# First loads on two queues in order of use, V's ones on GpSimd, and zero-adding matmuls from the first microseconds, in a gated pair of attention blocks

## The chip, the cores and the metric

One core of one Trainium2 chip runs the whole kernel. The metric is the time of one execution on the device in microseconds (us); several executions are timed and their median is quoted. The profile is one further execution, recorded; its span runs from the first instruction to the last and is about 2 us shorter than the time on the device (697.3 against 699.36 us for the kernel before).

In the profile PE is TensorE (PEld its weight loads), ACT is ScalarE, DVE is VectorE, POOL is GpSimd, SP is SyncE. SPq and ACTq are the instruction sequencers of SP and ACT, which issue transfers.

## The reference, cut

```python
# x: 2048 x 512; 32 heads of 16; bf16 inputs
g = sigmoid((x * gate_w).sum(-1, keepdims=True))
a = softmax(q k^T / 4) v  @ A_wo     # q, k, v from x @ A_wqkv, per head
b = linear attention(q', k', v') @ B_wo   # from x @ B_wqkv, phi(t) = t+1 or exp(t)
return g * a + (1 - g) * b
```

The softmax block decides the time. Its scores are handled in 2048 units, each 128 keys by 512 queries of one head (32 heads x 16 x 4). ScalarE takes two units at a time through a true exponential; VectorE (first step) and GpSimd or VectorE (two further steps) take the others through an approximation by integer arithmetic. TensorE makes the scores, multiplies the results with V, and makes all projections between them.

## The kernel before

The program is generated. Python code holds a list of tasks and candidate instructions, a model of how long each takes and when each buffer is there, and greedily emits the candidate that the model can start first. Each engine then runs its own instructions in the order emitted, with semaphore waits.

The first loads. The number after the semaphore's count in `dma` (4500.0) is a latency, and `issue` an issue time, that only the model uses; `tw` is the time at which the model counts data as there:

```python
for k3, kk in ((1, 0), (0, 1)):          # weights of K, then of Q, first 128 columns: ACT's queue
    dma(AC, wA0[:, :, k3, :], wsrc[...], semW0[k3], 16, 4500.0, writes=[r_wA0[k3]], issue=500.0)
for tb in range(4):                      # first 512 rows of x: SP's queue
    dma(SP, xnat[:, tb, :], x2[...], semX0[tb], 16, 3500.0, writes=[r_xn[tb]], issue=500.0)
dma(SP, wA0[:, :, 2, :], ...)            # weights of V
for t in range(1, NQC):                  # the other three blocks of x, transposed by the DMA, 4 pieces each
    for cc in range(NCC):
        dma(SP, xT[...], x2[...], semXT[t], 16 * NCC, 5500.0, transpose=True, issue=1300.0)
    for h in range(2):
        r_xT[t][h].w = _Raw(semXT[t], 16 * NCC)
        r_xT[t][h].tw = SP.free + 4200.0
# ... then gate weights, all of wA, wB, the rest of x, woA, woB on SP: 5.6 MB
```

The start and the filler:

```python
emit(DV, 1000, lambda: nc.vector.memset(Vc[:, 0], 1.0), writes=r_V)   # only columns 16, 17 of 18 must be one
emit(PE, 3400, [mm(...warm...) for b in range(9)], ...)               # nine 512-column matmuls on a zero tile
...
add_task(t_x0(), ...)                    # 16 transposes of the first x block on PE, two copies back (DVE, ACT)
add_task(t_k(0, 0, fixed=3), ...)        # first block of K, then of Q
add_task(t_q(0, 0, fixed=2), ...)
...
def fill_one(start, mode):               # in a gap of PE in the model, a matmul on the zero tile
    ...
    if n < 128 or PE.free < 20000.0:     # not in the first 20 us of the model
        return False
    ... mm(ps[...], warm[:, 0:128], warm[:, 0:n], start=lone, stop=lone)
```

The softmax here doesn't subtract the row's maximum and nothing guards it: scores larger than these inputs give would overflow.

## Time and profile before

The kernel before ran in 699.15 us (median of 3, 696.23 to 700.06).

| from the page | before |
|---|---|
| PE, ACT, DVE, POOL busy | 97%, 96%, 88%, 77% |
| exponentials on ACT | 706, 656.2 us |
| chain that ended last | PE 52%, ACT 32% |

The groups of instructions on ACT from 0 to 40 us and from 40 us on, before. Columns: line, engine, operation, tiles, shapes, count; busy time and mean of one; idle time of the engine just before them and who ended it.

```profile
L747 ACT ACTIVATE P<-ps 128x1024 bf16<-128x1024 f32 x21 | 20.2, 1025 | 11.4 <-PE ps L355 11.4
...
L747 ACT ACTIVATE P<-ps 128x1024 bf16<-128x1024 f32 x686 | 637.0, 1133 | 3.0 <-PE ps L355 3.0
```

In 650 us after the start the exponentials wait for TensorE for 3.0 us in all; in the first 40 us they wait 11.4 us, besides the first 9 us. So the first 40 us are the place to look. Busy time by stretches there, before. Columns: window, its length, busy us of PE, PEld, DVE, ACT, POOL with the number of instructions, granted clock of PE (1.00 is full), busy share of the DMA engines, GB/s.

```profile
0.00:10.00 10.00, 6.63 (x57) 2.96 (x58) 6.08 (x9) 3.08 (x4) 2.76 (x17) 1.00 0.63 150
10.00:20.00 10.00, 8.11 (x107) 2.70 (x107) 7.93 (x15) 6.93 (x8) 2.03 (x2) 0.58 0.51 101
20.00:30.00 10.00, 9.18 (x183) 3.60 (x181) 8.08 (x15) 7.51 (x8) 6.58 (x8) 0.91 0.89 318
30.00:40.00 10.00, 7.96 (x173) 3.25 (x177) 6.04 (x11) 5.32 (x6) 3.10 (x5) 1.00 0.82 264
```

The clock column shows half clock in most of 10 to 20 us (0.58 on average). The clock records in the trace give its limits: half clock from 11.61 to 21.85 us. The last stretch has another cause; here are two stalls of PE in it, before, from the timeline (start, length, engine, line, operation, tiles, count, and in brackets the idle time before and what ended it):

```profile
30.32 0.29 PE L361 MATMUL ps<-wA,xT 128*32 128x128 bf16 x7 [1.05 <-issue]
37.13 0.40 PE L361 MATMUL ps<-xT,T 128*32 128x512 bf16 x4 [1.72 <-issue]
```

"issue" means that the instruction waited for nothing that the profile records.

### The profile page before, as it was taken

Reading aid. Unit: us, or ns where it says so; the run is one execution under the profiler, and the core shown is the slowest. Engines: PE = TensorE matmul, PEld = TensorE weight load, DVE = VectorE, ACT = ScalarE, POOL = GpSimd, SP = SyncE. Lnnn points to the kernel's source line nnn. Section 1 sums busy time; section 2 is a strip of 40 time slices with the busy share of each in tenths; the row PEclk is TensorE's granted clock in tenths of the full one; section 3 lists DMA queues with packets and bytes.
Section 4 is the critical chain, followed back from the end, with each engine's and each line's share of the span. In section 5 each row is a group of like instructions: output and inputs, shape, how many; then the busy total and the mean of one; then the engine's idle time right before and its main releaser. Section 6 shows DMA issues by size and latency. Waiting matters only on the chain.

```text
span 697.3 us, 24196 instructions
## 1 busy us (share of the span) xinstructions
PE 679.6 (97%) x9919; PEld 205.4 (29%) x9919; DVE 614.4 (88%) x1089; ACT 668.5 (96%) x745; POOL 536.6 (77%) x597
## 2 busy tenths in 40 slices
PE   6999999999999999999999999999999999999998
PEld 2422332222322222222233323233333322222222
DVE  7788989889998888889889999889989898999985
ACT  4789999999999999999999999999999999999995
POOL 1569788887788887774797768887788888888792
PEclk8899999999999999999999999999999999999999
DMA  5810000000000000000000000000101111000001
GB/s 129 297 61 10 9 2 10 1 10 2 2 10 2 9 3 1 10 2 10 2 10 4 2 9 2 10 2 2 32 11 35 34 31 30 16 9 17 17 17 39
DMA packets 27869, 15.97 MB, mean 23 GB/s; under 512 B 19696, under 2 KB 26736, under 8 KB 27760
## 3 DMA queue, kind: packets, MB, share of 16 engines
q1 hardware_dynamic: 26704, 14.17, 7.6%
q8 instruction: 79, 1.29, 0.8%
q10 hardware_dynamic: 1056, 0.26, 0.2%
q14 instruction: 30, 0.25, 0.1%
HBM read 6.69 MB, written 2.10 MB: 13 GB/s over the span
## 4 chain that ended last, share of the span: by engine, by line
PE 52%; ACT 32%; issue 12%; DVE 2%; POOL 1%; ACTq 0%; DVEq 0%
PE ps L355 39%; ACT P L747 32%; PE ps L361 13%; POOL Z L720 1%; ACT eb L1020 1%; DVE Vc L421 0%; DVE Zbd L1054 0%; DVE KT L899 0%; DVE Qz L414 0%; ACTq L1404 0%; DVE gnat L977 0%; DVE Z L668 0%; DVE Qz L915 0%; DVE QT L921 0%; DVE mb L1021 0%
## 5 line engine op out<-in xcount | busy, mean ns | idle before, releaser
L747 ACT ACTIVATE P<-ps 128x1024 bf16<-128x1024 f32 x706 | 656.2, 1130 | 14.4 <-PE ps L355 14.4
L720 POOL TENSOR_TENSOR Z<-Z,mcon 128x512 int32<-128x512 int32 x411 | 423.7, 1056 | 100.3 <-DVE Z L668 65.4
L668 DVE TENSOR_SCALAR Z<-ps 128x512 int16<-128x512 f32 x637 | 427.0, 683 | 59.8 <-PE ps L355 53.6
L355 PE MATMUL ps<-Qz,KT 32*128 32x512 bf16 x2048 | 277.7, 387 | 5.7 <-ACT P L747 2.7
L355 PE MATMUL ps<-Z,Vc 128*17 128x512 bf16 x1911 | 277.6, 382 | 0.8 <-DVE T L985 0.5
L355 PE MATMUL ps<-P,Vc 128*17 128x512 bf16 x1411 | 256.6, 383 | 0.0
L355 PEld LDWEIGHTS ps<-Qz,KT 32*128 32x128 bf16 x2048 | 68.7, 91 | 267.4 <-ACT P L747 243.1
L725 DVE TENSOR_SCALAR Z<-Z 128x1024 int16<-128x1024 int16 x227 | 91.2, 435 | 0.5
L355 PEld LDWEIGHTS ps<-Z,Vc 128*17 128x17 bf16 x1911 | 63.6, 88 | 76.4 <-issue 48.4
L355 PE MATMUL ps<-warm 128*32 128x512 bf16 (+14 forms) x693 | 75.8, 333 | 1.4 <-POOL warm L406 1.4
L355 PEld LDWEIGHTS ps<-P,Vc 128*17 128x17 bf16 x1411 | 58.2, 88 | 52.5 <-issue 42.2
L361 PE MATMUL ps<-xT,wA 128*32 128x512 bf16 x512 | 45.7, 396 | 1.1 <-DVE xT L877 1.1
L1024 POOL TENSOR_TENSOR phiK<-eb,mb 128x512 bf16<-128x512 f32 x32 | 41.2, 1287 | 6.7 <-DVE Z L668 2.5
L952 POOL TENSOR_SCALAR Vc<-Vc 128x576 bf16<-128x576 bf16 x32 | 21.7, 680 | 15.0 <-DVE Vc L949 10.6
L1023 POOL TENSOR_SCALAR eb<-eb 128x512 f32<-128x512 f32 x32 | 19.8, 619 | 11.2 <-DVE Z L725 2.9
L355 PEld LDWEIGHTS ps<-warm 128*32 128x32 bf16 (+1 forms) x693 | 22.6, 95 | 18.8 <-issue 12.3
L985 DVE STREAM_TRANSPOSE T<-ps 128x512 f32<-128x512 f32 x32 | 22.7, 710 | 3.9 <-PE ps L361 2.1
L361 PE MATMUL ps<-wA,xT 128*32 128x128 bf16 x1024 | 23.1, 226 | 1.9 <-issue 1.1
L1008 POOL TENSOR_TENSOR T<-T,rg 128x256 bf16<-128x256 f32 x31 | 19.5, 628 | 5.4 <-DVE Z L668 1.8
L361 PE MATMUL ps<-woB,xnat 128*32 128x512 bf16 x256 | 23.3, 381 | 0.1
L1021 DVE TENSOR_SCALAR mb<-ps 128x512 f32<-128x512 f32 x32 | 21.8, 681 | 1.9 <-ACT eb L1020 0.5
L361 PE MATMUL ps<-wB,xT 128*32 128x512 bf16 x256 | 23.4, 382 | 0.0
(80 smaller groups left out, 313.5 us busy)
## 6 DMA issues: line engine op xcount, KB each, us to landing
Qz<-QT SPq DMA_DIRECT2D x120, 16.0 KB, 1.8
wA<-in_A_wqkv_dram SPq DMA_DIRECT2D x1, 1536.0 KB, 7.0
wB<-in_B_wqkv_dram SPq DMA_DIRECT2D x1, 1536.0 KB, 11.9
xnat<-in_A_x_dram SPq DMA_DIRECT2D x3, 512.0 KB, 13.1
out_dram<-outt SPq DMA_DIRECT2D x12, 128.0 KB, 1.7
xnat<-in_A_x_dram SPq DMA_DIRECT2D x4, 128.0 KB, 3.1
woA<-in_A_wo_dram SPq DMA_DIRECT2D x1, 512.0 KB, 9.4
woB<-in_B_wo_dram SPq DMA_DIRECT2D x1, 512.0 KB, 9.2
```

Of the source, the lines that this page charges most:

```text
L355: return lambda: nc.tensor.matmul(o, lhsT=l, rhs=r, start=start, stop=stop, skip_group_check=sg)
L361: h = nc.tensor.matmul(o[32 * j:32 * j + 32], lhsT=l[:, 32 * j:32 * j + 32], rhs=r, start=start, stop=stop, skip_group_check=True)
L668: return C(DV, 400, 533 * n + 74, lambda: nc.vector.tensor_scalar(o, i, ZB, 0.0, op0=ALU.add, op1=ALU.max), [r_bank[b] for b in bks], r_Z[ ...
L720: return C(PO, 400, 70 + 484 * n, lambda: nc.gpsimd.tensor_tensor(Z[:, z, 0:512 * n].bitcast(I32), Z[:, z0, 0:512 * n].bitcast(I32), mcon[ ...
L725: return C(DV, 450 if hot else 300, 69 + 134 * n, lambda: nc.vector.tensor_scalar(Z[:, z, 0:512 * n], Z[:, z0, 0:512 * n], float(m), None, ...
L747: return C(AC, 500, 427 * n + 49, lambda: nc.scalar.activation(P[:, slot, 0:512 * n], bank(b0, n), ACT.Exp, scale=ESC), [r_bank[b0 + k] fo ...
L952: yield po(690, lambda k=k: nc.gpsimd.tensor_scalar(Vc[:, k, vs].rearrange("p a b c -> p (a b c)"), Vc[:, 0, vs].rearrange("p a b c -> p ( ...
L985: yield dv(607, lambda: nc.vector.transpose(T1[:, a, :], bank(7)), [r_bank[7]], [r_T1[a]])
L1008: yield po(640, lambda: nc.gpsimd.tensor_tensor(t2[:, :, 16 * par:16 * par + 16], t1[:, :, 0:16], rg[:, a, :].unsqueeze(2).to_broadcast([1 ...
L1021: yield dv(607, lambda: nc.vector.tensor_scalar(mb[:, i, :], bank(b), 0.0, 1e-6, op0=ALU.max, op1=ALU.add), [r_bank[b], r_eb[i]], [r_mb[i]])
L1023: yield po(640, lambda: nc.gpsimd.tensor_scalar(eb[:, i, :], eb[:, i, :], 1.0, 0.0, op0=ALU.min, op1=ALU.max), [r_eb[i]], [r_eb[i]])
L1024: yield po(1300, lambda: nc.gpsimd.tensor_tensor(dst_ap, eb[:, i, :], mb[:, i, :], ALU.add), [r_eb[i], r_mb[i]], dst_res)
```

## The change

Its intent: the first x block, then the weights, arrive in the order in which they are used; the transposed loads start earlier, with more truthful latencies told to the model; VectorE is freed of a long memset; Q is projected before K so that Q's scaling overlaps; TensorE is kept active by zero-adding matmuls from 4.5 us of the model on. Core of the diff:

```diff
-        for k3, kk in ((1, 0), (0, 1)):
-            dma(AC, wA0[:, :, k3, :], ..., 4500.0, ..., issue=500.0)
-        for tb in range(4):
-            dma(SP, xnat[:, tb, :], ..., 3500.0, ..., issue=500.0)
-        dma(SP, wA0[:, :, 2, :], ..., 4500.0, ..., issue=500.0)
+        for E, tbs in ((SP, (0, 1)), (AC, (2, 3))):
+            for tb in tbs:
+                dma(E, xnat[:, tb, :], ..., 3300.0, ..., issue=450.0)
+        for k3 in (0, 1):
+            dma(AC, wA0[:, :, k3, :], ..., 3300.0, ..., issue=450.0)
         for t in range(1, NQC):
             for cc in range(NCC):
-                dma(SP, xT[...], ..., 5500.0, transpose=True, issue=1300.0)
+                dma(SP, xT[...], ..., 3900.0, transpose=True, issue=1300.0)
+            if t == 1:
+                dma(SP, wA0[:, :, 2, :], ..., 3500.0, ..., issue=450.0)
             for h in range(2):
-                r_xT[t][h].tw = SP.free + 4200.0
+                r_xT[t][h].tw = SP.free + 2900.0
...
-        emit(DV, 1000, lambda: nc.vector.memset(Vc[:, 0], 1.0), writes=r_V)
+        for p in range(NVQ):
+            emit(PO, 200, lambda p=p: nc.gpsimd.memset(Vc[:, 0, p]...[:, :, 16:18], 1.0), writes=[r_V[p]])
...
-        emit(PE, 3400, [mm(...) for b in range(9)], ...
+        emit(PE, 3000, [mm(...) for b in range(8)], ...
...
+        add_task(t_q(0, 0, fixed=2), -1, -1, "Q0,0")
         add_task(t_k(0, 0, fixed=3), -1, -1, "K0,0")
-        add_task(t_q(0, 0, fixed=2), -1, -1, "Q0,0")
...
-            if n < 128 or PE.free < 20000.0:
+            if n < 128 or PE.free < 4500.0:
```

More of the change, by code (lines that the diff above doesn't have):

```diff
@@ L380, in bass_gated_mix__mha_block__linear_attn_block__prompt_kernel @@
         out_fill = [0] * 6
-        for k3, kk in ((1, 0), (0, 1)):
-            dma(AC, wA0[:, :, k3, :], wsrc[:, :, k3 * D:k3 * D + 128], semW0[k3], 16, 4500.0, writes=[r_wA0[k3]], issue=500.0)
-        for tb in range(4):
-            dma(SP, xnat[:, tb, :], x2[128 * tb:128 * (tb + 1), :], semX0[tb], 16, 3500.0, writes=[r_xn[tb]], issue=500.0)
-        dma(SP, wA0[:, :, 2, :], wsrc[:, :, 2 * D:2 * D + 128], semW0[2], 16, 4500.0, writes=[r_wA0[2]], issue=500.0)
+        for E, tbs in ((SP, (0, 1)), (AC, (2, 3))):
+            for tb in tbs:
+                dma(E, xnat[:, tb, :], x2[128 * tb:128 * (tb + 1), :], semX0[tb], 16, 3300.0, writes=[r_xn[tb]], issue=450.0)
+        for k3 in (0, 1):
+            dma(AC, wA0[:, :, k3, :], wsrc[:, :, k3 * D:k3 * D + 128], semW0[k3], 16, 3300.0, writes=[r_wA0[k3]], issue=450.0)
         for t in range(1, NQC):
@@ L389, in bass_gated_mix__mha_block__linear_attn_block__prompt_kernel @@
                 dma(SP, xT[:, cc, 512 * t:512 * (t + 1)], x2[512 * t:512 * (t + 1), 128 * cc:128 * (cc + 1)], semXT[t],
-                    16 * NCC, 5500.0, transpose=True, issue=1300.0)
+                    16 * NCC, 3900.0, transpose=True, issue=1300.0)
+            if t == 1:
+                dma(SP, wA0[:, :, 2, :], wsrc[:, :, 2 * D:2 * D + 128], semW0[2], 16, 3500.0, writes=[r_wA0[2]], issue=450.0)
             for h in range(2):
                 r_xT[t][h].w = _Raw(semXT[t], 16 * NCC)
-                r_xT[t][h].tw = SP.free + 4200.0
+                r_xT[t][h].tw = SP.free + 2900.0
         dma(SP, gwc[:], gate_w.rearrange("(cc p) -> p cc", p=128), semG, 16, 3000.0, writes=[r_gw], noncontig=True, issue=500.0)
@@ L420, in bass_gated_mix__mha_block__linear_attn_block__prompt_kernel @@
              reads=[r_pidx], writes=[r_qmask])
-        emit(DV, 1000, lambda: nc.vector.memset(Vc[:, 0], 1.0), writes=r_V)
+        for p in range(NVQ):
+            emit(PO, 200, lambda p=p: nc.gpsimd.memset(Vc[:, 0, p].rearrange("p t h d -> p (t h) d")[:, :, 16:18], 1.0), writes=[r_V[p]])
         for k, m in enumerate(SHIFTS[1:]):
@@ L433, in bass_gated_mix__mha_block__linear_attn_block__prompt_kernel @@
                 reads=[rr], writes=[rr])
-        emit(PE, 3400, [mm(bank(b % 3 if b < 8 else 7), warm[:, 0:128], warm[:]) for b in range(9)], reads=[r_warm],
+        emit(PE, 3000, [mm(bank(b % 3 if b < 7 else 7), warm[:, 0:128], warm[:]) for b in range(8)], reads=[r_warm],
              writes=[r_bank[0], r_bank[1], r_bank[2], r_bank[7]])
```

## The prediction

> **What bounds the kernel now.** ScalarE's 706 exponentials take 656.2 us (group table); ACT is busy 96%, PE 97%; the chain that ended last is 52% PE, 32% ACT. From 40 to 690 us ACT is idle for under 5 us (busy time by stretches). Otherwise ACT's first exponential starts at 10.46 us, from 10 to 40 us ACT is busy for only about 20 us, and the tail is some 7 us. The change touches only the start.
>
> **The start (chain in order of time, timeline).** It runs through DVE: Qz memset (1.34 us), masks, Vc memset (2.94 us, from 3.62), then the xT copy (6.48), 32 projections (7.16 to 9.07), Qz scaling (9.13), first scores 10.03, first exponential 10.46. The last x block is issued on SP at 2.2 us and lands up to 3.5 us later; its transposes end on PE at 6.1.
>
> **What the change does there.**
> 1. Two x blocks go to ACT's queue: all four are issued by 1.3 us and land at about 4.6 us instead of 5.6. [...] here two issues of 0.45 us, and the order of arrival.
> 2. The Vc memset leaves DVE: six small POOL memsets instead, of 0.1 to 0.2 us each (a 128x128 one took 0.20). The xT copy can start with the last transpose: 0.4 us.
> 3. One warm matmul less (0.427 us apart).
> 4. Q before K: the 0.7 us Qz scaling runs during K's projection, the K cast (0.59 us) comes last: 0.5 us.
>
> Sum: first exponential near 8.9 us, 1.5 us earlier. Transposed loads start 1.4 us earlier on SP.
>
> **The clock.** The records show half clock from 11.6 to 21.85 us: 10.24 us[...]. From 16 to 22 us PE is nearly always busy at half clock, and exponentials wait (gaps 1.36, 0.85, 0.36 us). Zero-adding matmuls from 4.5 us should hold full clock: I estimate 2 us of ACT time, not 5, since K blocks 2 and 3 still wait for transposed loads that SP issues until 18 us.
>
> **What it doesn't touch.** From 22 to 38 us bulk loads run at up to 417 GB/s; PE stalls of 1.05 us (29.3) and 1.72 us (to 37.1), inside groups and marked "issue", and ACT gaps of 1.18, 2.48 and 3.14 us remain. I take them for instruction loads behind the bulk loads; they may swallow part of the gain. The whole later order is also rescheduled by the kernel's own model, which I expect to move the time by a few us either way.
>
> **Sum.** 1.5 + 2.0 + about 1 for earlier K blocks = 4.5 us of ACT time, nearly all critical, as ACT is hardly idle after 40 us. 699 - 4.5 = 694.5 us. The three runs before spread over 3.8 us.
>
> **What would show it.** First exponential at 8.5 to 9.3 us; clock 1.0 from 5 to 40 us; 15 to 40 more warm-tile matmuls before 20 us; DVE's memset gone; ACT busy 2 to 5 us more within the first 40 us; the same ACT rate beyond.
>
> **What would make it wrong.** The clock falling anyway; zero matmuls delaying scores; weights landing later than 6.3 us behind the transposed loads; the new order making ACT wait in the steady state; longer instruction stalls.
>
> Chances: faster by over 2% 0.03, within 2% 0.94, slower 0.03. Eight in ten: 689 to 700 us.

## The result, and the profile after

The changed kernel ran in 689.95 us (median of 4, 689.87 to 690.81), against 698.65 us of the kernel before (4 runs, 696.23 to 700.06). A ratio is the mean time of one kernel's runs over that of the other's of the same rounds, so not quite the ratio of the medians quoted: 0.9882, 95% interval 0.9852 to 0.9911. That is 1.2%, less than the 2% from which the prediction counts a kernel as faster. By the medians it is 8.7 us, inside the stated range but at its lower end, and nearly twice the 4.5 us that were worked out.

ACT from 0 to 40 us and from 40 us on, after:

```profile
L750 ACT ACTIVATE P<-ps 128x1024 bf16<-128x1024 f32 x29 | 27.3, 1046 | 4.5 <-PE ps L355 4.5
...
L750 ACT ACTIVATE P<-ps 128x1024 bf16<-128x1024 f32 x680 | 631.5, 1133 | 2.0 <-PE ps L355 2.0
```

Eight more exponentials were started by 40 us (29 against 21), and at 0.93 us apart (656.2 us over 706) eight of them are 7.4 us. The mean of one after 40 us is 1133 ns in both. So most of the gain is made in the first 40 us. The stretches, after:

```profile
0.00:10.00 10.00, 8.15 (x72) 3.48 (x72) 4.14 (x9) 3.41 (x5) 3.28 (x23) 1.00 0.77 157
10.00:20.00 10.00, 9.85 (x212) 3.97 (x210) 9.73 (x18) 10.00 (x12) 5.96 (x7) 1.00 0.43 95
20.00:30.00 10.00, 8.16 (x214) 3.81 (x206) 6.21 (x12) 7.51 (x8) 7.19 (x9) 1.00 0.94 333
30.00:40.00 10.00, 10.00 (x130) 2.73 (x126) 9.60 (x17) 8.47 (x10) 5.94 (x8) 1.00 0.79 255
```

PE runs at full clock from 4.81 us on, where its clock records begin (1.00). ACT gains 3.07 us in 10 to 20 us and 3.15 us in 30 to 40 us, and nothing between. Here is ACT's timeline, before and then after; each line is a run of instructions, and the bracket is the wait before it.

```profile
10.46 3.77 ACT L747 ACTIVATE P<-ps 128x1024 bf16<-128x1024 f32 x4 [1.61 <-PE ps L355]
14.62 1.02 ACT L747 ACTIVATE P<-ps 128x1024 bf16<-128x1024 f32 x1 [0.39 <-PE ps L355]
17.01 1.94 ACT L747 ACTIVATE P<-ps 128x1024 bf16<-128x1024 f32 x2 [1.36 <-PE ps L355]
19.80 1.94 ACT L747 ACTIVATE P<-ps 128x1024 bf16<-128x1024 f32 x2 [0.85 <-PE ps L355]
...
31.54 3.77 ACT L747 ACTIVATE P<-ps 128x1024 bf16<-128x1024 f32 x4 [2.48 <-PE ps L355]
38.45 3.77 ACT L747 ACTIVATE P<-ps 128x1024 bf16<-128x1024 f32 x4 [3.14 <-PE ps L355]
```

```profile
9.68 11.10 ACT L750 ACTIVATE P<-ps 128x1024 bf16<-128x1024 f32 x12 [0.50 <-PE ps L355]
21.00 1.94 ACT L750 ACTIVATE P<-ps 128x1024 bf16<-128x1024 f32 x2 [0.22 <-PE ps L355]
...
30.58 7.50 ACT L750 ACTIVATE P<-ps 128x1024 bf16<-128x1024 f32 x8 [1.05 <-PE ps L355]
39.03 3.77 ACT L750 ACTIVATE P<-ps 128x1024 bf16<-128x1024 f32 x4 [0.94 <-PE ps L355]
```

The first exponential comes only 0.78 us earlier, but then twelve follow each other without a gap, where before the fifth already had to wait. What opens the gaps is the second block of K: its cast on DVE, which makes new scores possible, before and then after:

```profile
15.60 0.69 DVE L899 CAST KT<-ps 128x512 bf16<-128x512 f32 x1 [0.29 <-PE ps L361]
```

```profile
12.28 0.68 DVE L902 CAST KT<-ps 128x512 bf16<-128x512 f32 x1
```

One of the two "issue" stalls is left after:

```profile
29.59 0.40 PE L361 MATMUL ps<-wA,xT 128*32 128x128 bf16 x14 [1.20 <-issue]
```

A finer measure, used below: for each trace, the time at which the n-th of the 2048 units had been through ACT's exponential (two units) or DVE's first step (one). The changed kernel is ahead of before by 0.8 us at unit 1, 2.8 at unit 20, 7.8 at unit 60 (32.6 against 40.4 us), 7.4 at unit 400, 9.8 at unit 1600 and 7.8 at the last. So 7.8 us are made by unit 60; after that the lead moves between 6.2 us (unit 100) and 9.8 us and ends where it was.

The spans differ by 9.2 us (697.3 against 688.1), and the missing 1.4 us are made in the tail, after the last unit: from there to the end of the span it is 9.87 us in the kernel before and 8.42 us in the changed one. All runs below that keep the exact order of one of the two have its tail to within 0.01 us, so this part belongs to the order of the last instructions.

### The profile page after: what moved, and what is told of

It is laid out like the page before. It is cut to its first block, busy times and chain, and to the rows that moved or that the text cites. A ratio compares the mean times of both kernels' runs of the same rounds, so it can differ in the third digit from the quotient of the medians.

```text
span 688.1 us, 24195 instructions
## 1 busy us (share of the span) xinstructions
PE 676.8 (98%) x9923; PEld 204.2 (30%) x9923; DVE 607.2 (88%) x1084; ACT 669.2 (97%) x746; POOL 536.8 (78%) x600
## 4 chain that ended last, share of the span: by engine, by line
PE 67%; ACT 20%; issue 8%; SPq 2%; DVE 1%; DMA 1%; POOL 0%; ACTq 0%; POOLq 0%
PE ps L355 52%; ACT P L750 19%; PE ps L361 15%; SPq L332 2%; ACT eb L1023 1%; DMA xT<-in_A_x_dram 1%; DVE Z L671 0%; POOL Z L723 0%; DVE Zbd L1057 0%; SPq L336 0%; DVE T L988 0%; ACTq L1407 0%; POOL T L1011 0%; ACT wA L1150 0%; POOLq L1407 0%
## 5 line engine op out<-in xcount | busy, mean ns | idle before, releaser
L355 PE MATMUL ps<-Z,Vc 128*17 128x512 bf16 x1902 | 269.8, 382 | 1.4 <-DVE T L988 1.1
L355 PE MATMUL ps<-P,Vc 128*17 128x512 bf16 x1414 | 246.2, 383 | 0.0
L355 PEld LDWEIGHTS ps<-Z,Vc 128*17 128x17 bf16 x1902 | 61.4, 88 | 71.4 <-issue 42.5
L355 PE MATMUL ps<-warm 128*32 128x512 bf16 (+18 forms) x703 | 76.3, 335 | 1.4 <-POOL warm L408 1.4
L355 PEld LDWEIGHTS ps<-P,Vc 128*17 128x17 bf16 x1414 | 55.8, 88 | 58.3 <-issue 45.8
L361 PE MATMUL ps<-xT,wA 128*32 128x512 bf16 x512 | 43.5, 383 | 0.9 <-DMA xT<-in_A_x_dram 0.6
L361 PE MATMUL ps<-xT,wB 128*32 128x512 bf16 x256 | 22.9, 383 | 0.0
L1023 ACT ACTIVATE eb<-ps 128x512 f32<-128x512 f32 x32 | 22.8, 714 | 0.0
```

The costliest lines, as they stand in the source:

```text
L355: return lambda: nc.tensor.matmul(o, lhsT=l, rhs=r, start=start, stop=stop, skip_group_check=sg)
L361: h = nc.tensor.matmul(o[32 * j:32 * j + 32], lhsT=l[:, 32 * j:32 * j + 32], rhs=r, start=start, stop=stop, skip_group_check=True)
L1023: yield ac(480, lambda: nc.scalar.activation(eb[:, i, :], bank(b), ACT.Exp), [r_bank[b]], [r_eb[i]])
```

## The experiments

Three explanations stood against each other. CLOCK: the zero-adding matmuls keep PE at full clock. LOADS: data lands earlier. ORDER: the scheduler, told other times, emits another order, above all the second K block sooner. They can be parted cleanly, because the zero-adding matmuls do not disturb the order of anything else, and because transfers can be moved between queues after the scheduler is done. A comparison of the emitted programs confirmed, for each run that says "exact order", that all other instructions of every engine kept their order; the traces show the same on PE, DVE, ACT and POOL, apart from moved memsets. Each run was timed in 5 rounds.

### 1. The zero-adding matmuls alone, on the order of before

```diff
-            if n < 128 or PE.free < 20000.0:
+            if n < 128 or PE.free < 4500.0:
```

> The kernel before with the change's last line alone: zero-adding matmuls allowed from 4.5 us of the kernel's own model on instead of from 20 us. The order of all other instructions on every engine stays exactly that of before. Theory CLOCK (most of the gain is that TensorE keeps full clock from 11.6 to 21.9 us): no half-clock stretch, 3 to 6 us faster than before (about 693 to 695). Theory ORDER (the gain comes from the new order of instructions that the scheduler makes when told of earlier loads): within 1 us of before although the clock holds. Theory LOADS (the gain comes from data that really lands earlier): within 1 us of before.

Measured: 694.74 us (693.71 to 695.07) against 698.11 us of before, ratio 0.9952 (0.9925 to 0.9978). The clock stays full in all six executions (mean granted clock 1.00), and in the profiled one the score matmuls between 9 and 23 us take 0.39 us each, where 24 of 32 in the kernel before take over 0.5. By units the run is 5.2 us ahead of before at unit 60 and 5.3 us at the last. ACT in the first 40 us:

```profile
L747 ACT ACTIVATE P<-ps 128x1024 bf16<-128x1024 f32 x27 | 25.5, 1036 | 6.4 <-PE ps L355 6.2
```

On the order of before, then, the clock is worth 3.4 us by the medians, within what CLOCK expected. How long the clock is at half differs from execution to execution. 33 executions of the kernel before were timed beside the runs:

| mean granted clock | executions | time |
|---|---|---|
| 1.000 | 3 | 694.23 to 694.64 us |
| 0.998 | 2 | 696.84 and 698.65 us |
| 0.995 | 11 | median 697.97 us |
| 0.993 | 17 | median 699.38 us |

So the kernel before with a full clock is as fast as this run, and about 4 us faster than its own median. The profiled execution had a mean clock of 0.993, which is why the profiles differ by more, 5.3 us of span.

### 2. The new start alone, on the order of before

After the scheduler is done, the emitted transfers are moved; the memset is cut to what matters but stays on DVE:

```diff
+        a_, s_ = [*AC.ops], [*SP.ops]; s_[2][1].eng = s_[3][1].eng = nc.scalar
+        AC.ops[:] = [s_[2], s_[3], a_[1], a_[0]]                 # x2, x3, weights of Q, of K
+        SP.ops[:] = [*s_[0:2], *s_[5:9], s_[4], *s_[9:]]         # x0, x1, 4 transposed, V's weights, rest
-        emit(DV, 1000, lambda: nc.vector.memset(Vc[:, 0], 1.0), writes=r_V)
+        emit(DV, 1000, lambda: nc.vector.memset(Vc[:, 0]...[:, :, 16:18], 1.0), writes=r_V)
```

> The kernel before in its exact order, with the start's physical work of the change: the first loads on two queues in the change's order, and the set-to-one of V cut from 3456 elements to the 384 that matter (left on DVE, so that no order changes). No early zero-adding matmuls. Theory LOADS: first exponential 0.7 to 1.5 us earlier, total 2 to 4 us faster (695 to 697). Theories CLOCK and ORDER: first exponential up to 1 us earlier, but at most 1.5 us in the total, since the half-clock stretch and the place of the second K block in the order remain.

Measured: 698.08 us (697.64 to 699.10), ratio 1.0003 (0.9973 to 1.0032). Nothing. The first exponential did not move either (10.47 us). PE from 6 us on in this run shows why:

```profile
7.18 1.91 PE L361 MATMUL ps<-xT,wA 128*32 128x512 bf16 x32 [1.14 <-DMA wA<-in_A_wqkv_dram]
```

In this order K is projected first, and K's weights are now last in ACT's queue, so the projections wait for them where they had waited for the copy of x; the start lost what it had won. And the second K block, whose x lands earlier here, cannot use that: it stands behind twelve score matmuls in PE's order. LOADS alone is refuted for this order and this sequence of loads; early loads with K's weights first were not tried.

### 3. Both, on the order of before

> Both of the former on the order of before: loads, short memset, early zero-adding matmuls. What is left against the changed kernel is only the order of instructions. Theory ORDER: at least 3 us slower than the changed kernel (693 or more). Theories CLOCK and LOADS: within 2 us of the changed kernel (690 to 692).

Measured: 694.14 us (693.85 to 695.19), ratio 0.9949 (0.9922 to 0.9976): like run 1. With the new start and the filler in place, 4.2 us to the changed kernel are left, and only the order (with one warm matmul, Q's place and the memset's engine) remains to make them. ORDER's expectation is met. Both kernels have a full clock in every execution, so these 4.2 us are not the clock's: in the profiles 2.7 us of lead are there at unit 60 (0.7 of them at the first exponential), and 1.4 us come in the tail.

### 4. The changed kernel without its early zero-adding matmuls

```diff
-            if n < 128 or PE.free < 4500.0:
+            if n < 128 or PE.free < 20000.0:
```

> The changed kernel with only its early zero-adding matmuls taken away (threshold back to 20 us); the order of all else stays exactly the same. Theory CLOCK: the clock falls to half for one or more windows before 22 us and the total grows by 3 us or more (693 to 696). Theories ORDER and LOADS: under 1.5 us slower (690 to 691.5), whether the clock falls or not.

Measured: 689.73 us (689.13 to 692.42), ratio to before 0.9892 (0.9862 to 0.9922). The profiled execution keeps full clock to the end and has 29 exponentials started by 40 us, as the changed kernel. CLOCK's expectation fails: in the new order the filler is worth nothing in the median. But two of the six executions took 692.18 and 692.42 us, and their mean clocks are 0.998 and 0.997, against 1.000 in the other four (689.13 to 689.90 us) and in all four of the changed kernel. So the clock did fall in those two, at a cost of some 3 us. When it fell is open, as neither was profiled, and so is whether the filler would have held it: in run 7, which has the filler, it fell after the stall at 28 us.

Stretch 8 to 12 us, first before, then this run (columns as above):

```profile
8.00:12.00 4.00, 2.32 (x29) 0.64 (x21) 2.84 (x5) 2.13 (x3) 0.00 (x0) 0.95 0.43 98
```

```profile
8.00:12.00 4.00, 2.96 (x40) 0.69 (x32) 3.42 (x7) 2.90 (x4) 0.00 (x0) 1.00 0.56 128
```

With the second K block among the first scores PE is busy 2.96 of these 4 us instead of 2.32, and the clock holds by itself in the profiled execution. So the filler and the new order are not two gains that add up: in most executions the order keeps the clock without the filler. That PE's activity in this stretch is the reason fits the runs that were asked for it (before and run 2, whose clock falls at the end of the stretch, have PE busy for 2.32 and 2.33 of the 4 us; runs 4, 5 and 1 and the changed kernel, whose clock stays full, for 2.96, 3.05, 3.32 and 3.50), but was not varied by itself in the new order. The clock records go further. The half-clock stretches before the programs' ends last 3.41 us (runs 8 and 10) or a multiple of it (6.83 in run 7, 10.24 in the kernel before), so the "windows" of the expectation above are read as 3.41 us each. In the traces of the kernel before and of the changed one the time at full clock was cut into pieces of 3.41 us, from each rise of the clock. Three of the 400 pieces have PE busy for less than 1.75 us: 1.73 us in the one before the fall at 11.61 us, 0.20 and 1.21 us in the last piece of each program; half clock follows all three. The other 397, with 1.79 us or more, are followed by full clock. The same count over all 11 traces that have clock records has exceptions: of 19 pieces with 1.74 us or less 18 end with the clock at half (12 of the 19 lie at the end of the program; the other seven all end with a fall), and of the 2182 with more, 2 do. No single long pause precedes the fall at 11.61 us: the longest idle time of PE in the 6.8 us before it was 1.07 us. In this run the 3.41 us from 8.25 us on have 2.40 us.

### 5. One number told to the scheduler of before

```diff
-                r_xT[t][h].tw = SP.free + 4200.0
+                r_xT[t][h].tw = SP.free + 1700.0
```

> The kernel before with one number changed: its scheduler is told that transposed blocks of x land 2.5 us earlier than it thought (the time at which it counts them there goes from 4200 to 1700 ns after the issue). No load, no memset, no zero-adding matmul is changed; only the order of instructions follows. Theory ORDER: the second K block goes right behind the first scores, the first exponential stays at 10.46 us, and the total falls by 3 to 7 us (692 to 695.5), with or without a shorter half-clock stretch. If the order pays only with the loads moved as well, it stays within 1.5 us of before, with waits of TensorE on the transposed loads.

Measured: 693.14 us (692.43 to 693.56), ratio 0.9919 (0.9904 to 0.9933). With the loads, the memset and the filler of before, a number that no engine ever sees makes 5.5 us of the 8.7. The second K block's cast and the first exponentials in this run:

```profile
12.47 0.68 DVE L899 CAST KT<-ps 128x512 bf16<-128x512 f32 x1
10.75 10.19 ACT L747 ACTIVATE P<-ps 128x1024 bf16<-128x1024 f32 x11 [1.61 <-PE ps L355]
```

The clock stays full from 6.08 us to the end of the work, in the other five executions too (mean clock 1.00), and the run is 6.1 us ahead of before at unit 60. Its first exponential came 0.3 us later, because the clock rose at 6.08 us and not at 4.79: the 16 transposes of the first x block took 1.49 us instead of 1.10 (up to 314 ns each instead of 219). Against the executions of the kernel before that also kept a full clock (694.23 to 694.64 us) this run gains about 1.3 us, and against run 1 (694.74 us) 1.6. So most of the 5.5 us is the clock, which this order keeps without a filler, and the rest is the order itself.

### 6. The changed kernel with the loads of before

The transfers are moved back in the same way, the order of the rest is exact.

> The changed kernel in its exact order, early zero-adding matmuls included, but with the first loads issued on the queues and in the sequence of before (the scheduler is not told). Theory NEED (the new order lives on data that lands earlier): TensorE waits about 1 us more for the second block of K and the last one, and the total grows by 1 to 2.5 us, to 691 to 692.5. Theory FREE (the loads were never waited for; only the order counts): within 0.5 us of the changed kernel, 689.5 to 690.5.

Measured: 691.00 us (690.13 to 691.40), ratio 0.9886 (0.9870 to 0.9902). 1.05 us slower than the changed kernel by the medians, at the lower edge of what NEED expected and above FREE's. The two sets were timed at different times, their ranges overlap (the changed kernel's is 689.87 to 690.81 us), and the ratios to before are nearly equal (0.9886 and 0.9882). The first exponential comes at 10.01 us instead of 9.68, but not because of the loads. The transposes of the first x block start at the same time in both and only take longer, first the changed kernel, then this run:

```profile
4.76 1.09 PE L878 MATMUL ps<-identb,xnat 128*128 128x128 bf16 x16
4.75 1.43 PE L878 MATMUL ps<-identb,xnat 128*128 128x128 bf16 x16
```

In run 6 the first six took 311 ns each and the last eight 219 ns, as all but the first of the changed kernel do: the clock rose during them. The other difference is the PE stall at 28 us, 2.04 us long instead of 1.20. These two are as large as the whole difference of the spans (1.05 us), so that earlier loads are worth anything in the new order is not shown.

### 7. The changed kernel with the long memset on VectorE

> The changed kernel in its exact order, but with V set to one by the single 3456-element memset on VectorE instead of six small ones on GpSimd. If the memset gates the start, the first copy of x starts about 0.6 us later, the first exponential comes at about 10.3 instead of 9.68 us and the total grows by 0.6 us (690.5). If something else gates the start (the ScalarE copy of the other half of x, the weights), nothing moves: 690.0.

Measured: 691.76 us (690.31 to 694.29), ratio 0.9903 (0.9882 to 0.9924). The first exponential comes at 10.21 us, 0.53 us later, as expected if the memset gates. DVE's copy of x starts at 6.48 us, behind the memset, instead of 5.88. The times are spread in a way that this cannot explain, but the mean clocks can: only the two quickest executions, 690.31 and 690.59 us, kept a full clock; the other four (691.76 to 694.29 us) have 0.995 to 0.998. In the profiled one (693.64 us) the clock was at half from 31.62 to 38.45 us (0.66 on average in 30 to 40 us), after a PE stall of 1.84 us at 28.24. The two with a full clock are 0.4 to 0.6 us above the changed kernel's median, though within its range (to 690.81 us). The memset's price is read from those and the first exponential as about 0.5 us; the rest of the median is the clock.

### 8. The whole load section, told to the scheduler, on the kernel before

> The kernel before with the change's load section whole: queues, sequence, and the times told to the scheduler; K before Q, the memset on VectorE and the threshold of 20 us stay. Theory ORDER: like the run in which the scheduler alone is told, within 1.5 us of it. Theory NEED: at least 1.5 us faster than that run, and no wait of TensorE on transposed loads before 15 us.

Measured: 695.80 us (695.01 to 699.16), ratio 0.9962 (0.9940 to 0.9985). Neither theory had this: slower than run 5, although the loads really are earlier. At unit 40 it is 4.6 us ahead of before; then PE stalled for 1.81 us at 30.05 us and its clock was at half from 32.86 to 36.27 us in the profiled execution (0.83 in 30 to 40 us), and again for 6.8 us at 568.8 us (0.50 in 570 to 575 us); all six executions have mean clocks below 1.000 (0.993 to 0.998). The second fall is explained by the next two runs.

### 9. and 10. The same number, a little different

1800 and 1100 ns in place of the 1700 of run 5. (Told 1300, 1400, 1500 or 1600 ns, the scheduler ran into a dead end and built no program; the same happened when Q's place in the changed kernel, or all times in the kernel before with its loads kept, were varied alone. So Q before K could not be tried by itself.)

> As b_told (one number told to the scheduler of the kernel before), with 1800 ns in place of 1700: a difference of 0.1 us in the model that makes another order from the second K block on. If the start of the order makes the gain and the rest is equal: within 1.5 us of b_told's 693.1. If chance in the later order is as large as the gain: 3 us or more away.

> As b_told with 1100 ns: the scheduler puts the second K block even before the first scores, so that TensorE must wait for the transposed loads, which in this kernel land as late as before. Too early a time told costs a wait of 0.5 to 1 us before the first scores; else as b_told: 693 to 695. 3 us or more away from b_told for other reasons would show how much the later order varies by chance.

Measured: 696.45 us (695.37 to 697.92) and 698.38 us (697.57 to 699.01), ratios 0.9974 (0.9946 to 1.0001) and 1.0001 (0.9977 to 1.0025). Both missed the expectation of staying near run 5. At unit 400 all three are equally far ahead of before: 5.4, 5.3 and 5.4 us. At unit 1600 the two are 8.3 and 7.2 us ahead, at unit 1800 only 1.9 and 0.7. The loss is one event (a half-clock stretch of 3.41 us at 382.86 us in the run with 1100 ns, whose mean clock is 0.993, leaves no mark in the units). DVE and PE in the run with 1800 ns, from the timeline:

```profile
567.84 0.69 DVE L1108 TENSOR_TENSOR wA<-ps,wA 128x512 bf16<-128x512 f32 x1 [3.44 <-DMA xnat<-wA]
568.59 1.05 PE L361 MATMUL ps<-xT,wA 128*32 128x512 bf16 x8 [3.56 <-DVE wA L1108]
```

and what SP's queue issued in front of that transposing copy:

```profile
561.44 3.75 SPq L336 DMA_DIRECT2D Qz<-QT  x6
565.23 4.59 SPq L332 DMA_TRANSPOSE xnat<-wA  x3
```

DVE needs a buffer that a transposing copy must first empty; that copy is issued at 565.23 us, behind six small copies of Q in SP's queue that took 3.75 us to issue (0.6 us each, against a median of 1.8 us from issue to landing of such a copy in the kernel before), and lands some 2.6 us later; PE, which works in order, stops 3.56 us, and then its clock is at half from 567.30 to 574.13 us (0.73 on average in 565 to 570 us, 0.59 in 570 to 575 us). By the units on either side the whole costs about 6 us. The same wait of PE (3.56 and 3.62 us at 566 us) is in run 8 and in the run with 1100 ns. The kernel before, the changed one and run 5 have no such collision there: their PE is never idle for more than 0.3 us from 550 to 600 us. In the changed kernel such a copy stands behind eight copies of Q as well:

```profile
561.49 4.94 SPq L336 DMA_DIRECT2D Qz<-QT  x8
566.48 1.27 SPq L332 DMA_TRANSPOSE xnat<-wA  x1
```

But nothing waits for it there. So it is the place of the waiting instructions in the order that makes the loss, not the queue alone; this is read from the traces, and no run moved the copies. This is the chance in the later order, and it is as large as the gain.

### 11. and 12. The big loads later

Wanted as a test of the "issue" stalls at 28 to 37 us, on both kernels in exact order. Of the 5.6 MB that are loaded from 19 us on, 4.1 MB are needed only after 70 us:

```diff
+        SP.ops[:] = [*SP.ops[:17], *SP.ops[23:31], *SP.ops[17:23], *SP.ops[31:]]   # wB, x, woA, woB behind 8 copies of Q
```

> The changed kernel in its exact order, but the big loads that nothing needs before 70 us (second weight matrix, rest of x, both output weights, 4.1 of the 5.6 MB loaded from 19 us on) are issued on SP behind the first eight small copies of Q, at about 42 us. Theory FETCH (TensorE's stall of 1.2 us at 28.4 us, and ScalarE's gaps there, come from instruction loads that queue behind these loads): the stall at 28 us is gone, the instruction loads come at even distances, ScalarE is idle 2 to 4 us less between 20 and 40 us, and the total falls to 686.5 to 688.5 us. Theory ORDER STALL (something else in the order holds TensorE there): stall and total stay (689.5 to 690.5).

> The same edit on the kernel before, in its exact order, with its loads, memset and half-clock stretch. Theory FETCH: its TensorE stalls of 1.05 us (29.3) and 1.72 us (35.4) go, the total falls by 2.5 to 4.5 us, to 694 to 696. If the stalls have another cause: 698 to 699.

Measured: on the changed kernel 688.87 us (687.88 to 689.09), ratio to before 0.9863 (0.9840 to 0.9887); on the kernel before 696.13 us (694.63 to 696.49), ratio 0.9966 (0.9942 to 0.9991). From 27 to 39 us PE is never idle for more than 0.1 us any more. The instruction loads are visible as single packets of 16,384 bytes in a queue of their own; that they are PE's is inferred from their number, 79 for PE's 19,838 instructions in the trace. They started at 14.6, 19.7, 27.3 and 33.8 us in the changed kernel, the third after PE had begun 900 instructions of the trace, 347 after the second; with the bulk loads away they started at 15.0, 20.0, 25.7 and 29.9 us, the third 303 instructions after the second. ACT in the first 40 us of the changed kernel with late bulk loads:

```profile
L750 ACT ACTIVATE P<-ps 128x1024 bf16<-128x1024 f32 x30 | 28.0, 1069 | 2.7 <-PE ps L355 2.7
```

FETCH holds: the stall goes with the loads, in both kernels. The traces of the two kernels tie it to the instruction packets too: their three PE stalls of over 0.2 us between 27 and 38 us (1.05, 1.72 and 1.20 us) end 1.48, 1.53 and 1.30 us after the end of such a packet; over the 12 traces with bulk loads it is 14 stalls and 1.22 to 1.55 us. Runs 1 and 3, which have the bulk loads as well, stall there for 0.22 and 0.34 us. The gain of 1.1 us on the changed kernel is below the 1.5 to 3.5 us expected; the two sets of runs do not overlap, but the ratios' intervals do, so this is the fastest version measured, and by a margin that the intervals do not secure. In the kernel before the gain is 2.7 us, as expected. There the clock may have a part in it: the one execution of run 12 with a full clock took 694.63 us, no less than the three of the kernel before (694.23 to 694.64).

## Why the prediction was right or wrong

**The place was right for most of it.** The gain was expected in the first 40 us, and 7.8 us of the 9.2 between the profiles are made there; the steady state is unchanged (1133 ns per exponential in both). The other 1.4 us come in the tail, where the prediction expected no change. Of the signs that it named, the clock stayed at 1.0, 17 more warm-tile matmuls ran before 20 us, and DVE's long memset is gone. Two were missed: the first exponential (9.68 us against 8.5 to 9.3) and ACT's busy time in the first 40 us, 6.5 us more (29.4 against 22.9) instead of 2 to 5.

**The size was off, and the terms of the sum were off in different directions.** Predicted were 1.5 us for the first exponential, 2.0 us for the clock, 1 us for earlier K blocks, together 4.5 us; measured 8.7 us. The time fell inside the stated range because that is 11 us wide; the sum reached only half of the gain.

- *First exponential, 1.5 us.* It came at 9.68 us, 0.78 us earlier (the clock rose at 4.8 us in both profiles). 0.53 us of that are there when the projections start (6.63 against 7.16 us), where x loads, memset and warm matmul were to give about 1. "Q before K" was credited with 0.5 us and gave 0.26: from the last projection to the first score matmul it is 0.69 us instead of 0.95, as the cast of K that now comes last (0.59 us) is nearly as long as the scaling that it replaces (0.70 us for the first half). The x blocks landed even a little earlier than predicted (the last at 4.3 us), but the early loads did not help by themselves: run 2 has them and no earlier exponential. The memset (about 0.5 us, run 7) was priced well.
- *Clock, 2.0 us, "not 5".* This is the term that was mis-sized most. "Zero-adding matmuls from 4.5 us should hold full clock there": they do, and on the order of before that is worth 3.4 us by the medians (run 1), about 4 us by the kernel before's own executions, and 5.2 us at unit 60 in the profiles. The reason given for the low figure, that K blocks still wait for transposed loads, did not hold: in run 1, with the loads of before, the third and fourth K block are cast at 20.02 and 24.88 us instead of 22.71 and 27.30. And the filler is not the only thing that keeps the clock: the new order does so without it in four of six executions (run 4), and the told order in all six (run 5).
- *Earlier K blocks, "about 1".* With a full clock in both, the changed order is 2.7 us ahead of run 3 at unit 60, and 0.7 of that is the first exponential: about 2 us for this term. Telling the scheduler alone brings the second K block 3.1 us sooner (run 5); the exponentials do not wait for it, and PE, denser (3.05 us busy in 8 to 12 us against 2.32), keeps its clock. The prediction saw the new order only as a disturbance that would "move the time by a few us either way", and did not ask what the model's numbers would do to PE's order at 10 us.

**What of the 8.7 us is settled.** With the clock full on both sides 4.2 us are left (run 3 against the changed kernel): 2.7 us at the start, in which the first exponential's 0.7 us are contained, and 1.4 us in the tail. The rest (4.5 us as the difference, 3.4 us in run 1) is the clock, which either the filler (run 1) or the order (run 5) holds. One told number gives 5.5 us (run 5), most of it by keeping the clock. The short memset is worth about 0.5 us (run 7); the filler nothing in the median of the new order (run 4). Whether the earlier loads are worth anything is not shown (runs 2 and 6). Q before K, one warm matmul less and the later order were not parted. That later order is a matter of luck: it decided between 693 and 698 us for kernels that differ in one told number (runs 5, 9, 10), and it gave the changed kernel its shorter tail.

**What the prediction said would stay.** The stall at 29 us stayed (1.20 us) and its cause, named as a supposition, is confirmed by runs 11 and 12. Of the two long ACT gaps after 30 us, 2.48 and 3.14 us, 1.05 and 0.94 us are left: the second PE stall (1.72 us) did not come back, as PE had by then fewer instructions left of the dense kind. That last reason is argued, not shown.

## What to carry to other kernels

In a program whose order comes from a model, the times told to the model are part of the tuning: correct them against the trace first, before moving any work. But compare several orders, as 1700, 1800 and 1100 ns gave 693.1, 696.5 and 698.4 us. Test an order by keeping it exact while moving the physical cause. Compare kernels by when the n-th unit of work is done, not by the total alone: the same early gain of about 5.4 us ended as 5.5, 2.4 or 0.5 us by the medians because of one collision 500 us later. Look at the mean clock of every execution before a spread is called noise: here it parts 694 from 699 us for one and the same kernel. Put early loads that nothing needs for long behind what is needed: here, moving 4.1 MB that were needed only after 70 us took away PE stalls of 1.20 us in the changed kernel and of 1.05 and 1.72 us in the kernel before, and 1.1 and 2.7 us of the medians (runs 11 and 12).
